# Where x's transposed tiles come from: TensorE transposes of the centred tile, or a DMA that adds a stored transposed layout onto a broadcast of negative means

## The chip, the cores and the metric

The kernel runs on one core of one Trainium2 chip, in one launch. The metric is device time in microseconds, the median of several runs. Beside it there is one profiled execution with its trace. Engines are named as in the profile: PE is TensorE's matmul side and PEld its weight loads, DVE is VectorE, ACT is ScalarE, POOL is GpSimd, SP is the engine that here only issues DMAs. "SPq" or "ACTq" stands for the queue of an engine that issues DMAs and waits.

## What is computed

x has 2048 rows of 512. Its rows are normalised, and two mixers work on the same normalised rows; their results are added to x:

```python
xn = _layernorm(x, axis=-1)                 # (x - m) / sqrt(v + 1e-5), per row
return x + _A_ref(xn, wqkv, w_phi, wo) + _B_ref(xn, w_in, w_sp, b_sp, w_out)
# A: q, k, v = xn @ wqkv, 32 heads of 16; p = q or k @ w_phi per head;
#    phi = [softmax(p), softmax(-p)]; kv = phi_k^T v; z = sum of phi_k;
#    o = (phi_q kv) / (phi_q z + 1e-6); result o @ wo
# B: z = gelu(xn @ w_in), halves z1 and z2; g = w_sp @ layernorm(z2) + b_sp;
#    result (z1 * g) @ w_out
```

Only the way in which xn reaches TensorE is touched. The mean is subtracted from x ahead of the matmuls; the factor 1/sqrt(v + eps), `r_x`, is applied to their results.

## The kernel before

**Precision.** Every matmul is made in three: each operand is split into a rounded part h (`round_h`, line 47, on ACT) and a rest l (`rest_l`, line 51, on DVE), and `mm3` (lines 53 to 57) adds h·h, h·l and l·h in PSUM. These helpers are used all over the kernel, so lines 47, 51, 55, 56 and 57 stand in the profile for many different steps; the tiles' names tell them apart.

**Rows and stages.** The 2048 rows are 16 tiles of 128, counted 0 to 15; "the fifth tile" is tile 4. The first stage, which ends a little after 200 us, makes for each tile the projections to q, k and v (`proj`, 12 matmuls of 512 columns each), the paired softmax of q and of k on DVE and ACT (`softmax_pair`), the sums over k and v (`add_kv`, where matmuls for several tiles are put together after tiles 3, 7, 11, 13 and 15), and the first half of the gated mixer's input (`z1_raw`, 24 matmuls of 344 columns). Later come the other half with its layer norm, the large product with `w_sp` (`products`), and the output projections. All of that follows the first stage and is not edited.

**How x reaches TensorE.** TensorE contracts over the partitions, so it needs x tiles with the 512 features on the partitions, as four blocks of 128×128. For tile s the steps are, in the kernel before:

- `fetch(s)`, `load_x` (line 179): SP loads 128×512 of x (256 KB) into `xt[s]`, one of XB = 5 buffers.
- `stats` (lines 260, 261): DVE takes mean and variance. `neg_mean` (line 265): POOL makes `nm`, minus the mean, one number for each row. `rstd_of` (lines 92, 93): POOL makes `r_x`.
- `center` (line 269): ACT adds `nm` to the tile, in place. Rows are partitions here, so this is a bias for each partition.
- `transposed` (line 275): PE transposes four blocks into the PSUM tile `pt`, one of the four PSUM buffers of the tag "mm" that the projections use too.
- `split_x` (lines 47 and 51): ACT and DVE read `pt` from PSUM and write the h and l halves of `xT[s]`.

Tiles 0 to 3 are made ahead of the loop, in an order written out by hand. From tile 4 on the loop over s does it: iteration s calls `centered(s + 2)`.

**What sets the order.** Each engine works through its own list in order and waits where an operand is not there. The lists are written before the program runs, by a planner that plays the program through with durations of its own: `TileContext(nc, schedule_with_timeline_sim=True)` in the last lines of the kernel. Among the instructions that it thinks ready on an engine it takes the one that stands first in the program. `tc.issue_after(i)` adds a rule that the instructions in its block come after i on i's engine. So an edit in one place can change the lists everywhere, and a wait that the planner thought shorter stops an engine at that place, with all that is queued behind it. The input `x_t` holds x's tiles already transposed, as (tile, feature in block, block, row); the kernel before takes it as an argument and does not use it.

Of the kernel before, what the change touches and what calls it, by code (L numbers as in the profile page):

```python
# [10 lines left out]
F32 = mybir.dt.float32  # L11
F32R = mybir.dt.float32r
AF = mybir.ActivationFunctionType
ALU = mybir.AluOpType
# [4 lines left out]
P = 128  # L19
S, D, H, DH, FH = 2048, 512, 32, 16, 688  # L20
NT = S // P
ND = D // P
# [6 lines left out]
BL = 32  # L29
EPS_LN = 1e-5  # L30
EPS_DEN = 1e-6
XB = 5
NP = NT // 2
HP, QP = P // 2, P // 4
FP = 3 * P
# [4 lines left out]
def mixer(ctx: ExitStack, tc: tile.TileContext, x, x_t, wv, wqkT, phi_bd, wo, w_in, wst, b_r, w_out, out):  # L40
    nc = tc.nc
    pe, act, dve, pool, sp = nc.tensor, nc.scalar, nc.vector, nc.gpsimd, nc.sync


    def round_h(eng, h, src):
        if eng is act:
            return act.activation(h, src, AF.Copy).ins  # L47
        return eng.tensor_copy(h, src).ins

    def rest_l(l, src, h, eng=None):  # L50
        return (eng or dve).tensor_tensor(l, src, h.bitcast(F32), op=ALU.subtract).ins  # L51
# [18 lines left out]
    def xz_tile(n, dt, name):  # L70
        return xz.tile([P, SL], dt, tag="xz", name=name)[:, :n]

    mid = ctx.enter_context(ExitStack())
    dram = ctx.enter_context(tc.tile_pool(name="dram", bufs=1, space=DRAM))
# [2 lines left out]
    u_d = dram.tile([NT, FU, P], F32, name="u_d")  # L77
    kvT_d = dram.tile([P, D], F32, name="kvT_d")
    zb_d = dram.tile([P, NF], F32, name="zb_d")

    ident = cst.tile([P, P], F32, name="ident")
    make_identity(nc, ident)
# [6 lines left out]
    def rstd_of(mv, r, stats=None):  # L89
        if stats is not None:  # L90
            dve.bn_aggr(mv, stats)
        pool.tensor_scalar_add(mv[:, 1:2], mv[:, 1:2], EPS_LN)
        pool.tensor_tensor(r, mv[:, 1:2], mhalf, op=ALU.pow)
# [52 lines left out]
    def z1_raw(pl, ps, s, bufs):  # L146
        z = pl.tile([P, 2, FC], F32, tag="zf", bufs=bufs, name="z1f")
        for k, p in zproj(ps, s, w1):
            act.activation(z[:, k], p, AF.Copy, scale=r_x[:, s:s + 1])
        act.dma_start(z1_d[s], z.rearrange("p a b -> p (a b)"))  # L150
# [21 lines left out]
    with ExitStack() as p0:  # L172
        res = p0.enter_context(left("p0res", 1))
        wk = p0.enter_context(left("p0wk", 2))
        ps = p0.enter_context(psum("p0ps", 4))

        def load_x(s):
            t = wk.tile([P, D], F32, tag="x", bufs=XB, name="xt")
            sp.dma_start(t, x[s * P:(s + 1) * P, :])
            return t  # L180
# [24 lines left out]
        def fold(i, wT, tiles):  # L205


            for g in range(NG):
                for c in range(ND):
                    for m in range(2):  # L210
                        for r in range(2):
                            rows, cols = slice(r * HP, (r + 1) * HP), slice(m * HP, (m + 1) * HP)
                            ins = pe.matmul(tiles[c // 2][r][cols, c % 2, g], wT[g][rows, c * P + m * HP:c * P + (m + 1) * HP],
                                            bd[rows, g * P + r * HP:g * P + (r + 1) * HP], start=True, stop=True,
                                            skip_group_check=True).ins
            return ins

        def folded(i, tiles, keep=lambda **ins: None, between=lambda: None):
            for k in range(2):
                if k:  # L220
                    between()
                for r in range(2):
                    h, l = (w[:, i, 2 * k:2 * k + 2].rearrange("p c (g a b) -> p c g a b", g=NG, a=2)[:, :, :, r] for w in (wqk_h, wqk_l))
                    keep(act=round_h(act, h, tiles[k][r]))
                    keep(dve=rest_l(l, tiles[k][r], h))

        def fold_tiles(pools):
            return [[pl.tile([P, D], F32, tag=tag, name="fold").rearrange("p (c g b) -> p c g b", c=2, g=NG)
                     for _ in range(2)] for pl, tag in pools]
# [15 lines left out]
        xt, v, rounded, ready = {}, {}, [], []  # L245

        def fetch(s):
            if s < NT:
                xt[s] = load_x(s)

        def split_x(src):
            t = xz_tile(2 * D, F32R, "xT").rearrange("p (a b) -> p a b", a=2)
            xT.append(t)
            src = src.rearrange("p a b -> p (a b)")
            rounded.append(round_h(act, t[:, 0], src))
            return rounded[-1], rest_l(t[:, 1], src, t[:, 0])

        def stats(s, keep=lambda **ins: None):
            st6 = wk.tile([P, 6], F32, tag="st6", name="st6")
            dve.bn_stats(st6, xt[s])  # L260
            keep(dve=dve.bn_aggr(mv_x[:, s], st6).ins)

        def neg_mean(s):
            nm = wk.tile([P, 1], F32, tag="nm", name="nm")
            pool.tensor_scalar_mul(nm, mv_x[:, s, 0:1], -1.0)
            return nm

        def center(s, nm):
            return act.activation(xt[s], xt[s], AF.Identity, bias=nm).ins

        def transposed(s):
            xs = xt.pop(s)
            pt = ps.tile([P, ND, P], F32, tag="mm", name="pt")
            for c in range(ND):
                ins = pe.transpose(pt[:, c], xs[:, c * P:(c + 1) * P], ident).ins
            return pt, ins

        def centered(s):
            stats(s)
            nm = neg_mean(s)  # L280
            rstd_of(mv_x[:, s], r_x[:, s:s + 1])
            with tc.issue_after(rounded[s - 2]):
                center(s, nm)
            split_x(transposed(s)[0])

        def keep_v(s, p):
            v[s] = wk.tile([P, D], F32, tag="v", bufs=4, name="v")
# [2 lines left out]
        def proj_v(s):  # L290
            keep_v(s, proj(s, wv_h, wv_l))
# [4 lines left out]
        def proj_k(s):  # L296
            er = spare[s].rearrange("p a b -> p (a b)")[:, :NF + 2 * H] if s in spare else None
            return softmax_pair(wk, proj(s, wqk_h[:, 1], wqk_l[:, 1]), "k", r_x[:, s:s + 1], er=er)

        def proj_q(s):  # L300
            e = softmax_pair(wk, proj(s, wqk_h[:, 0], wqk_l[:, 0]), "q", r_x[:, s:s + 1])
            pool.dma_start(e_d[s], e)

        def add_kv(s, er):

            e = er[:, :NF]
            dve.tensor_tensor(heads(e), heads(e), bc(er[:, NF:], 2 * H), op=ALU.mult)
            pool.dma_start(zacc, e, accum_op=ALU.add)
            ready.append((v.pop(s), e))
            if s not in RUNS:  # L310
                return
            first = s == RUNS[0]
            with ExitStack() as later:
                n = len(ready)
                while ready:
                    vs, e = ready.pop()
                    for m in range(H // 2):
                        k = m % 4 * QP
                        i = pe.matmul(kv_acc[k:k + QP, m // 4], vs[:, m * QP:(m + 1) * QP], e[:, m * HP:(m + 1) * HP],  # L319
                                      start=first and m < 4 and len(ready) == n - 1, stop=s == NT - 1 and not ready,  # L320
                                      skip_group_check=True).ins
                    later.enter_context(tc.issue_after(i))
# [17 lines left out]
        def keep(**ins):  # L340
            for i in ins.values():
                queue.enter_context(tc.issue_after(i))
# [17 lines left out]
        nm = neg_mean(1)  # L360
# [12 lines left out]
        def split_t(pt):  # L373
            i, j = split_x(pt)
            keep(act=i, dve=j)


        t = xz_tile(2 * D, F32R, "xT").rearrange("p (a b) -> p a b", a=2)
# [8 lines left out]
        for cs, pt in zip(halves, pts):  # L387
            src = pt.rearrange("p a b -> p (a b)")
# [23 lines left out]
        def settled(s):  # L412
            stats(s, keep)
            nm = neg_mean(s)
            rstd_of(mv_x[:, s], r_x[:, s:s + 1])
            return nm

        nm = settled(2)
# [4 lines left out]
        nm = settled(3)  # L423
# [24 lines left out]
        keep(pe=zproj.last)  # L448
        spare.update(zip((2, 3, 4, 5, 8, 9), [bd_t] + wkT_t + wqT_t[:1] + w1r))
        n1, nq = 1, 0  # L450
        for s in range(NT):
            fetch(s + 4)
            er = ek[s] if s < len(ek) else proj_k(s)
            if 1 < s < NT - 2:
                centered(s + 2)
            while nq < (s - 2) * NT // (NT - 3):
                proj_q(nq)
                nq += 1
            add_kv(s, er)
            if s == 0:  # L460
                tiles = fold_tiles(((za, "z"), (ps, "mm")))
                keep(pe=fold(0, wqT, tiles))
                folded(0, tiles)
            elif s == 1:
                proj_v(3)
            elif 2 < s < NT - 1:
                proj_v(s + 1)
            while n1 < s * (NT - LAG) // (NT - 1):
                z1_raw(wk, za, n1, 2)
                n1 += 1  # L470
            if s == 3:
                queue.close()
# [330 lines left out]
    for n in range(NC):  # L803
# [27 lines left out]
        if n == NC - 2:  # L831
            es[0], es[1] = first_q(0), first_q(1)
            t = xz_tile((KF + 1) * P, F32R, "u1")
# [10 lines left out]
    wk = ctx.enter_context(left("cwk", 2))  # L844
# [187 lines left out]
```

## Time and profile before

| | us |
|---|---|
| median of 3 runs | 629.55 |
| lowest and highest run | 628.14, 629.68 |
| the profiled execution's own time | 627.78 |
| its span, first to last instruction | 626.1 |
| PE busy | 619.1 (99%) |
| DVE busy | 508.8 (81%) |
| ACT busy | 280.7 (45%) |
| POOL busy | 104.8 (17%) |

The span is what the views of the trace divide up; the profiled execution's own time is 1.7 us more. It lies 1.77 us under the median of the runs. The granted clock of TensorE is 0.999 over the span. Busy shares are averages over stages that have different limits, so a stage is read from its own stretch of the trace.

### The profile page before, as it was taken

The page shows a single profiled execution, that of the slowest core. Times are in us where ns is not written, and L with a number is a line of the kernel's source. Part 1 is how long each engine was busy: PE and PEld are TensorE (multiplying, and loading weights), DVE is VectorE, ACT ScalarE, POOL GpSimd, SP SyncE. Part 2 cuts the span into 40 slices and gives each one's busy share as a digit, 9 for nine tenths or more (in the row PEclk, how much of TensorE's full clock was granted, in tenths as well). Part 3 has the DMA queues.
Part 4 walks back from the last instruction along what each step waited for, and adds up shares of the span by engine and source line. Part 5 has one row for each costly group of instructions (what it writes and reads, how often), then busy time and mean ns, then how long its engine had stood idle before and what let it go on. Part 6 is the DMA issues. An engine that isn't in the chain of part 4 may idle for free.

```text
span 626.1 us, 11429 instructions
## 1 busy us (share of the span) xinstructions
PE 619.1 (99%) x4406; PEld 565.3 (90%) x4406; DVE 508.8 (81%) x893; ACT 280.7 (45%) x446; POOL 104.8 (17%) x187
## 2 busy tenths in 40 slices
PE   8999999999999999999999999999999999999996
PEld 7888888888888999999999999999999877788775
DVE  5999998987988398989898897696978899989211
ACT  5653434443333367877434444243445433334331
POOL 4142122111011015442000000000000212211110
PEclk9999999999999999999999999999999999999999
DMA  9445465354336868001454845637367799984722
GB/s 313 164 109 144 121 156 155 88 143 136 104 93 173 274 234 285 2 2 35 147 115 147 193 96 153 136 119 175 88 174 232 224 297 330 320 249 97 180 34 51
DMA packets 87590, 98.40 MB, mean 157 GB/s; under 512 B 46560, under 2 KB 59616, under 8 KB 87296
## 3 DMA queue, kind: packets, MB, share of 16 engines
q1 hardware_dynamic: 75200, 58.12, 32.4%
q0 software_dynamic: 10032, 33.92, 20.7%
q10 hardware_dynamic: 2304, 5.64, 2.4%
q8 instruction: 34, 0.56, 0.4%
q14 instruction: 20, 0.16, 0.1%
HBM read 56.37 MB, written 30.54 MB: 139 GB/s over the span
## 4 chain that ended last, share of the span: by engine, by line
PE 98%; DVE 0%; ACT 0%; POOL 0%; issue 0%; DVEq 0%; POOLq 0%
PE g L57 11%; PE g L56 11%; PE g L55 11%; PE proj L57 7%; PE proj L55 7%; PE proj L56 7%; PE zps L57 6%; PE zps L55 6%; PE zps L56 6%; PE pout L55 5%; PE pout L57 5%; PE pout L56 5%; PE ptq L890 1%; PE po L905 1%; PE kvps L319 1%; PE pout L919 1%
## 5 line engine op out<-in xcount | busy, mean ns | idle before, releaser
L56 PE MATMUL g<-B,A 128*128 128x344 f32 x448 | 143.3, 320 | 0.0
L55 PE MATMUL g<-B,A 128*128 128x344 f32 x448 | 142.8, 319 | 0.0
L57 PE MATMUL g<-B,A 128*128 128x344 f32 x448 | 140.6, 321 | 0.1
L55 PEld LDWEIGHTS g<-B,A 128*128 128x128 f32 x448 | 84.3, 188 | 0.0
L56 PEld LDWEIGHTS g<-B,A 128*128 128x128 f32 x448 | 84.2, 188 | 0.0
L57 PEld LDWEIGHTS g<-B,A 128*128 128x128 f32 x448 | 83.6, 188 | 0.4 <-DVE A L51 0.4
L47 ACT ACTIVATE A<-S 128x512 fp32r<-128x512 f32 x64 | 39.4, 630 | 71.3 <-DVE S L542 51.3
L55 PE MATMUL proj<-wqk_h,xT 128*128 128x512 f32 x128 | 50.6, 395 | 0.0
L57 PE MATMUL proj<-wqk_h,xT 128*128 128x512 f32 x128 | 50.2, 393 | 0.0
L56 PE MATMUL proj<-wqk_l,xT 128*128 128x512 f32 x128 | 49.9, 390 | 0.0
L47 ACT ACTIVATE A<-wf 128x512 fp32r<-128x512 f32 (+1 forms) x64 | 33.2, 521 | 36.3 <-DMA wf<-in_wst 14.3
L119 ACT ACTIVATE e<-e,r_x 128x1024 f32<-128x1024 f32 x26 | 29.9, 1150 | 40.2 <-DVE e L118 39.6
L51 DVE TENSOR_TENSOR A<-S,A 128x512 fp32r<-128x512 f32 x64 | 43.1, 686 | 4.8 <-ACT A L47 4.3
L55 PE MATMUL zps<-w_0h,xT 128*128 128x344 f32 x128 | 41.4, 323 | 0.0
L57 PE MATMUL zps<-w_0h,xT 128*128 128x344 f32 x128 | 41.0, 320 | 0.0
L55 PE MATMUL zps<-w_1h,xT 128*128 128x344 f32 x128 | 40.9, 320 | 0.0
L57 PE MATMUL zps<-w_1h,xT 128*128 128x344 f32 x128 | 40.7, 319 | 0.0
L56 PE MATMUL zps<-w_0l,xT 128*128 128x344 f32 x128 | 40.6, 317 | 0.0
L56 PE MATMUL zps<-w_1l,xT 128*128 128x344 f32 x128 | 40.6, 317 | 0.0
L51 DVE TENSOR_TENSOR A<-wf,A 128x512 fp32r<-128x512 f32 (+1 forms) x64 | 35.0, 549 | 2.6 <-ACT A L47 2.4
L707 POOL DMA_DIRECT2D z1t<-z_d x16 | 8.7, 547 | 165.5 <-DMA u_d<-z1t 98.7
L122 DVE TENSOR_REDUCE sm<-e 128x64 f32<-128x1024 f32 x26 | 31.4, 1207 | 5.1 <-ACT e L119 5.0
(205 smaller groups left out, 1432.7 us busy)
## 6 DMA issues: line engine op xcount, KB each, us to landing
wf<-in_wst SPq DMA_DIRECT2D x64, 256.0 KB, 3.4
e_d<-e POOLq DMA_DIRECT2D x16, 544.0 KB, 4.6
et<-e_d SPq DMA_DIRECT2D x16, 544.0 KB, 6.4
er<-et POOLq DMA_DIRECT2D x12, 512.0 KB, 6.4
z_d<-z1f ACTq DMA_DIRECT2D x16, 344.0 KB, 2.6
z1t<-z_d POOLq DMA_DIRECT2D x16, 344.0 KB, 5.2
zacc<-e POOLq DMA_DIRECT2D x10, 512.0 KB, 4.7
u<-u_d SPq DMA_DIRECT2D x15, 320.0 KB, 5.6
```

The lines of the kernel that those rows point to most:

```text
L47: return act.activation(h, src, AF.Copy).ins
L51: return (eng or dve).tensor_tensor(l, src, h.bitcast(F32), op=ALU.subtract).ins
L55: pe.matmul(dst, ah, bh, start=start, stop=False)
L56: pe.matmul(dst, ah, bl, start=False, stop=False)
L57: return pe.matmul(dst, al, bh, start=False, stop=stop).ins
L119: act.activation(e, e, AF.Exp, scale=scale)
L122: dve.tensor_reduce(sm, heads(e), axis=AX.X, op=ALU.add)
L319: i = pe.matmul(kv_acc[k:k + QP, m // 4], vs[:, m * QP:(m + 1) * QP], e[:, m * HP:(m + 1) * HP], start=first and m < 4 and len(ready) == n ...
L707: pool.dma_start(t[:, k, :FH], z1_d[2 * i + k])
L890: pe.transpose(pt[:, a, k].bitcast(F32R), src, ident_r)
L905: lasts[3] = pe.matmul(po[r][c * QP:(c + 1) * QP, k], kvT[rows, m // 2, cols], fs[m // 4][rows, m // 2 % 2], start=True, stop=True).ins
L919: lasts[2] = pe.matmul(p, rt, w, start=False, stop=i == NT - 1 and k == 1).ins
```

## The change

For tiles 4 to 15, x is no longer centred and transposed on the engines. DVE takes the statistics as before. SP stores the 128 negative means of a tile in a row of the DRAM tensor `nm_d`. A second SP DMA reads that row back and writes it to all 128 partitions and all four blocks of a new tile `xc[s]`, 128×512. POOL then issues a DMA that adds the stored transposed layout `x_t[s]` onto `xc[s]`. ACT and DVE split `xc[s]` from SBUF. The buffers of `xt` go from 5 to 3, and `xc` has two. `center_t(s + 4)` runs in iteration s, two iterations ahead of its `split_x`, and its statistics are put after the last `rest_l` of `split_x` on DVE. The loads of x are called one iteration earlier. Tiles 0 to 3 are made as before.

```diff
-XB = 5
+XB = 3
...
+    nm_d = dram.tile([NT, P], F32, name="nm_d")
...
             rounded.append(round_h(act, t[:, 0], src))
-            return rounded[-1], rest_l(t[:, 1], src, t[:, 0])
+            split_x.last = rest_l(t[:, 1], src, t[:, 0])
+            return rounded[-1], split_x.last
...
-        def centered(s):
-            stats(s)
+        xc = {}
+
+        def center_t(s):
+
+            with tc.issue_after(split_x.last):
+                stats(s)
+            xt.pop(s)
             nm = neg_mean(s)
             rstd_of(mv_x[:, s], r_x[:, s:s + 1])
-            with tc.issue_after(rounded[s - 2]):
-                center(s, nm)
-            split_x(transposed(s)[0])
+            sp.dma_start(nm_d[s].unsqueeze(1), nm)
+            xc[s] = wk.tile([P, ND, P], F32, tag="xc", name="xc")
+            sp.dma_start(xc[s], nm_d[s].unsqueeze(0).unsqueeze(0).to_broadcast([P, ND, P]))
+            pool.dma_start(xc[s], x_t[s], accum_op=ALU.add)
...
+        fetch(4)
         for s in range(NT):
-            fetch(s + 4)
+            fetch(s + 5)
             er = ek[s] if s < len(ek) else proj_k(s)
             if 1 < s < NT - 2:
-                centered(s + 2)
+                split_x(xc.pop(s + 2))
+            if s < NT - 4:
+                center_t(s + 4)
```

## The prediction

> **What bounds the kernel now.** I read the page's engine totals first, then a table by stretch for the first stage and what follows it, then the chain of work that ended last.
>
> ```profile
> PE 619.1 (99%) x4406; PEld 565.3 (90%) x4406; DVE 508.8 (81%) x893; ACT 280.7 (45%) x446; POOL 104.8 (17%) x187
> ```
>
> ```profile
> 25.00:60.00 35.00, 35.00 (x417) 30.80 (x415) 34.85 (x60) 16.52 (x25) 11.77 (x26) 1.00 0.48 112
> 60.00:100.00 40.00, 40.00 (x201) 34.56 (x200) 37.98 (x59) 15.92 (x21) 8.92 (x18) 1.00 0.47 133
> ...
> 230.00:300.00 70.00, 70.00 (x445) 70.00 (x444) 61.34 (x125) 52.55 (x80) 29.05 (x50) 1.00 0.28 94
> ```
>
> ```profile
> 25.00:205.00 180.00, 180.00 (x1503) 156.66 (x1501) 163.02 (x245) 72.31 (x96) 36.11 (x67) 1.00 0.47 129
> ```
>
> The columns are the stretch, its length, then busy time of PE, PEld, DVE, ACT and POOL with instruction counts, granted clock, DMA share and GB/s. From 25 to 205 us, where the change acts, PE is busy in all of the 180 us: TensorE is the limit, at full clock. DVE has 163.02 of 180, so 17 us to spare, but nearly none early: 34.85 of 35 up to 60 us, and 2.0 of 40 free up to 100. DMA is at half. From 230 to 300 us PE is again busy throughout, and over the whole span it idles for only 626.1 − 619.1 = 7 us. So PE time taken out of the first stage comes off the end, as long as PE stays fed, and little more than that can be won.
>
> **What is removed: 48 transposes.** For twelve tiles four transposes each go. What they cost PE is read from the start times, not from the durations.
>
> ```profile
> 87.85 0.39 PE L56 MATMUL proj<-wqk_l,xT 128*128 128x512 f32 x1
> 88.08 0.40 PE L57 MATMUL proj<-wqk_h,xT 128*128 128x512 f32 x1
> 88.31 0.60 PE L275 MATMUL pt<-ident,xt 128*128 128x128 f32 x4
> 88.67 0.48 PE L55 MATMUL proj<-wqk_h,xT 128*128 128x512 f32 x1
> 88.98 0.39 PE L56 MATMUL proj<-wqk_l,xT 128*128 128x512 f32 x1
> ```
>
> Matmuls of 512 columns start every 0.23 us (87.85, 88.08). From 88.08 to 88.98 two such steps and the four transposes pass: 0.90 − 2×0.225 = 0.45 us, part of it the slower first matmul behind them. The chain that ended last puts 0.44 us on each quartet, first and last of the twelve:
>
> ```profile
> 38.13 0.44 PE pt L275 x4
> ...
> 165.59 0.44 PE pt L275 x4
> ```
>
> So the saving is 12 × 0.45 = 5.4 us of PE time, all of it on the limiting path.
>
> ```profile
> L275 PE MATMUL pt<-ident,xt 128*128 128x128 f32 x60 | 9.0, 272 | 0.0
> L47 ACT ACTIVATE xT<-pt 128x512 fp32r<-128x512 f32 x15 | 8.9, 594 | 19.7 <-PE pt L275 19.7
> L51 DVE TENSOR_TENSOR xT<-pt,xT 128x512 fp32r<-128x512 f32 x15 | 10.1, 672 | 1.9 <-ACT xT L47 1.9
> L269 ACT ACTIVATE xt<-xt,nm 128x512 f32<-128x512 f32 x15 | 10.6, 713 | 0.5 <-POOL mv_x L92 0.5
> L47 ACT ACTIVATE wv_h<-wrow 128x512 fp32r<-128x512 f32 x4 | 2.4, 628 | 0.2 <-DMA wrow<-in_wv 0.2
> L51 DVE TENSOR_TENSOR wv_l<-wrow,wv_h 128x512 fp32r<-128x512 f32 x4 | 2.7, 688 | 0.1
> ```
>
> One transpose lasts 272 ns by its own row, but the next starts well before it ends. The Trainium skill, "TensorE: Matmul & The Clock Gate", Part 4, gives about 275 ns for a 128×128 transpose in one kernel's context; the duration here agrees, and priced by it 48 would be 13.2 us. Here four of them with the weight load behind delay the next start by 0.36 us (88.31 to 88.67), so the pitch decides, not the duration.
>
> Twelve centrings of 0.713 us leave ACT, 8.6 us of an engine that is busy 72 of 180: no gain of its own. The split reads SBUF instead of PSUM; the weight splits from SBUF took 628 and 688 ns against 594 and 672, so 12 × 0.016 = 0.2 us more on DVE, inside its 17 us. DVE does not get less work. A PSUM buffer that was held by each `pt` is free for projections; PE waits for none now, so I count nothing.
>
> **What is added.** Per tile two SP DMAs, one POOL DMA and three transfers, one after the other. Nothing like the 4-byte-per-partition store or the broadcast is in the trace, so I bound them by rows; the columns are the size of one and the median time to landing:
>
> ```profile
> xt<-in_x SPq DMA_DIRECT2D x16, 256.0 KB, 3.9
> wf<-in_wst SPq DMA_DIRECT2D x64, 256.0 KB, 3.4
> zacc<-e POOLq DMA_DIRECT2D x10, 512.0 KB, 4.7
> u<-u_d SPq DMA_DIRECT2D x15, 320.0 KB, 5.6
> out<-xr POOLq DMA_DIRECT2D x15, 256.0 KB, 5.8
> kvT_d<-kvT SPq DMA_DIRECT2D x1, 256.0 KB, 3.3
> wof<-in_wo SPq DMA_DIRECT2D x16, 64.0 KB, 2.8
> bias<-in_b_r SPq DMA_DIRECT2D x1, 8.0 KB, 7.2
> ```
>
> Store of `nm`: between 2.8 (64 KB) and 7.2 us (`bias`, 128 short rows amid the first weights); I take 3.3, the store of `kvT`, also 128 partitions to DRAM. Broadcast: between 3.4 and 5.6 (`u`, whose runs are 512 bytes like these); I take 3.9, the x load of the same size. Adding DMA: between 3.4 (a plain load of the size) and 5.8 (one that adds in DRAM); I take 4.7, `zacc`, which adds in SBUF. Sum 11.9 us, between 9.6 and 18.6. The Trainium skill, "DMA: Bandwidth & Descriptors", "Anatomy of one DMA", gives about 2.0 us plus bytes/436e3 for one DMA; estimated by that, the three would take 2.0 + 2.6 + 2.6 = 7.2 us. That is for GpSimd DMAs by themselves; the 256 KB loads here took 3.4 to 3.9 against its 2.6, so the rows decide.
>
> Does the chain keep PE waiting? The tightest place is the first new tile, because its statistics must now follow the split of tile 3 on DVE.
>
> ```profile
> 28.64 0.68 DVE L51 TENSOR_TENSOR xT<-pt,xT 128x512 fp32r<-128x512 f32 x1
> ```
>
> ```profile
> 45.95 0.39 PE L55 MATMUL proj<-wv_h,xT 128*128 128x512 f32 x1
> ```
>
> ```profile
> 69.76 0.39 PE L55 MATMUL proj<-wv_h,xT 128*128 128x512 f32 x1
> ```
>
> ```profile
> L260 DVE BATCH_NORM_STATS2 st<-xt 128x6 f32<-128x512 f32 x16 | 10.7, 680 | 6.7 <-DMA xt<-in_x 6.7
> L261 DVE BATCH_NORM_AGGREGATE mv_x<-st 128x2 f32<-128x6 f32 x16 | 2.7, 172 | 0.2
> L265 POOL TENSOR_SCALAR nm<-mv_x 128x1 f32<-128x1 f32 x15 | 3.5, 234 | 34.6 <-DVE mv_x L261 24.2 <-ACT xt L269 9.9
> L122 DVE TENSOR_REDUCE sm<-e 128x64 f32<-128x1024 f32 x26 | 31.4, 1207 | 5.1 <-ACT e L119 5.0
> L308 POOL DMA_DIRECT2D zacc<-e x10 | 9.1, 909 | 60.9 <-DVE e L307 30.1 <-DVE e L123 27.4 <-ACT wqk_h L47 2.3
> ```
>
> The first row is the rest of tile 3, which ends at 29.32. From there: statistics 0.68 + 0.17, `nm` 0.23, transfers 11.9, split 0.63 + 0.69 = 14.3, so tile 4 is split at 43.6 us, with the bounds 41.3 and 50.3. PE first uses it in the fifth run of twelve `wv` matmuls, at 45.95, or 45.05 with the two quartets ahead of it gone. So it comes in time by 1.4 us on my values and 5.3 us late at worst, once. I count zero and keep 0 to 5.3 for the range. Afterwards there is room: tile 6 follows tile 4 by the same 14.3 us, at about 58 us, and its `wv` run (the seventh) starts at 69.76. The two buffers of `xc` let odd and even tiles run side by side, so the chain gives a tile every 7 us where PE takes 180/16 = 11.
>
> The queues: SP has nothing in the first stage but the x loads, and each next load is called ahead of the waiting DMAs. With XB = 3 tile 3's load waits for the transposes of tile 0, over at 6.03, and is issued at 10.09 anyway:
>
> ```profile
> 4.97 1.06 PE L384 MATMUL pt<-ident,xt 128*128 128x128 f32 x4
> ```
>
> ```profile
> 10.09 0.33 SPq L179 DMA_DIRECT2D xt<-in_x  x1
> ```
>
> POOL's adding DMA waits for the broadcast, and behind it stand the writes of q's exponentials, the sums into `zacc` and the next tile's `nm` and `r_x`. POOL is busy 36 of 180 us; twelve issues of 0.9 us (as `zacc`'s, the last row above) and twelve waits of at most 3.9 + 3.3 us, if it comes to each straight after `nm`, are 97 us of the 144 free. In its rows it waits for DVE, 30.1 and 27.4 us before the `zacc` sums. Cover: POOL's idle time; without it the k and q buffers would come free late, up to 7 us each. Traffic: 12 × 512 KB in 180 us, 35 GB/s on 129.
>
> **The sum.** 627.78 − 5.4 = 622.4 us for the profiled execution, which stands 1.77 us below the median of its runs; for the median, 629.55 − 5.4 = 624.1 us.
>
> **The rivals.** *ACT stands at the rounding (slower).* The lists are fixed beforehand. If the planner takes the transfers as shorter than they are, ACT stops at `round_h` of `xc` with an exponential queued behind it, and DVE stops at the sum of that exponential. For it: DVE's four waits for an x load in its rows come to 6.7 us, 1.7 us late for each transfer, so some 5 us over three in a row; DVE has no idle time up to 60 us. If DVE bridges 2.4 us of that with another softmax's work, two steps of 1.2 us as the sum `sm` takes, it loses 2.6 us a tile: 163 + 12 × 2.6 = 194 us against 180, +14 us, 644. It cancels the gain from 1.0 us a tile (163 + 12 = 175, PE's new length) and makes it slower from 1.4 on. Against: the steps are called two iterations, 2 × 11 us, ahead of the split, and such waits so far stopped no PE. *The gain is spent on the first tile (no change).* The chain takes its upper bound, PE waits 5.3 us at tile 4 before it can start, 629.4 us; a DVE loss of 1.0 to 1.4 us a tile ends there too. For: only 1.4 us margin, on a store that no row shows. Against: the planner may move other matmuls ahead. *The transposes cost their duration:* 48 × 0.272 = 13.1 us, 616.5. Against: the start times above, and PE has no idle time to hide such a cost.
>
> **How the numbers follow.** About 0.3%, 1.9 us, is what a measurement of this kernel can tell from no change. Forecast 0.62, within 622 to 627. No change or a part of the gain 0.18, of which a quarter is still faster by 1.9 us. ACT's stand 0.18, anywhere from 631 to 645. Full durations 0.02. Faster 0.62 + 0.04 + 0.02 = 0.68, same 0.14, slower 0.18. The range 622 to 634 leaves out the transposes' full price, a little of the forecast's low side, and the upper two thirds of ACT's stand, near 0.16.
>
> **What would show it.** Right: 16 transposes in the rows instead of 64 (four each for tiles 0 to 3), PE still busy throughout from 25 us on, its total down by about 5.4 us, tile 4's `wv` run near 45 us with no idle time ahead, the three transfers near 3.3, 3.9 and 4.7 us, and the stage's last `kvps` matmuls 5 us earlier. Wrong: PE idle before `proj<-wv` waiting for `xT`; ACT waiting for a DMA at line 47 and DVE for ACT in the sums, by more than 1 us a tile; or POOL's wait turning up as DVE's.

## The result and the profile after

The changed kernel takes 753.0 us (median of 5 runs, 750.29 to 753.6) where the kernel before took 628.22 on the same chip: 1.197 times as long, with a 95% interval from 1.195 to 1.199. The forecast was 624.1 us, in a range from 622 to 634. The profiled execution took 751.65 us, its span is 749.9. Three executions further down, one of e7 (741.8 us), one of e9 (1223.4) and the profiled one of e10 (1558.1), were slower than the others of their kernel and are left out of the times, and no landing of e10 is used.

First the engine totals and two rows of the table in 40 slices of the page of the changed kernel. A slice is 18.7 us.

```profile
PE 639.2 (85%) x4358; PEld 576.8 (77%) x4358; DVE 508.1 (68%) x893; ACT 272.2 (36%) x434; POOL 117.0 (16%) x199
...
PE   8936356238249989999999999999999999999997
...
PEclk9978658669758999999999999999999999999999
```

From the third to the twelfth slice, 37 to 225 us, PE is busy for 2 to 8 tenths; from the thirteenth on it runs nearly as before. In the same stretch the granted clock goes down to between 0.5 and 0.9, where before it was full throughout. So PE's total went up by 20 us although 48 matmuls are gone: the same matmuls last longer at a lower clock. That goes with the idling: e4 below, which keeps PE busy in the same stage, has full clock in it. It is taken here as a consequence, because the waits below account for the idling.

The table by stretch, with the columns as before:

```profile
25.00:60.00 35.00, 22.63 (x219) 19.20 (x218) 16.34 (x27) 6.63 (x11) 7.48 (x13) 0.80 0.49 101
60.00:100.00 40.00, 18.74 (x79) 15.97 (x78) 13.76 (x22) 5.35 (x7) 4.85 (x9) 0.75 0.32 58
100.00:200.00 100.00, 52.36 (x315) 42.40 (x313) 38.15 (x62) 14.29 (x19) 15.70 (x26) 0.74 0.54 78
```

From 60 to 100 us PE issues 79 matmuls where it issued 201, and no engine is busy for half of the time: DVE has 13.76 of 40, POOL 4.85. Nothing computes too slowly; everything waits. The groups of instructions and the waits say for what (idle time of the engine ahead of the instruction; in the waits total, times, longest):

```profile
L51 DVE TENSOR_TENSOR xT<-xc,xT 128x512 fp32r<-128x512 f32 x12 | 8.1, 684 | 95.2 <-ACT xT L47 95.2
...
L47 ACT ACTIVATE xT<-xc 128x512 fp32r<-128x512 f32 x12 | 7.3, 626 | 115.6 <-DMA xc<-in_x_t 115.6
```

```profile
POOL xc L292 <- DMA xc<-nm_d: 161.7, 12, 19.4
ACT xT L47 <- DMA xc<-in_x_t: 115.6, 8, 20.6
...
DVE xT L51 <- ACT xT L47: 97.2, 10, 17.5
```

DVE waits for ACT, ACT for the adding DMA, and POOL, which issues that DMA, for the broadcast. The DMA issues (KB each, median us to landing) give the lengths:

```profile
xt<-in_x SPq DMA_DIRECT2D x16, 256.0 KB, 5.3
...
xc<-nm_d SPq DMA_DIRECT2D x12, 256.0 KB, 9.6
xc<-in_x_t POOLq DMA_DIRECT2D x12, 256.0 KB, 4.3
...
nm_d<-nm SPq DMA_DIRECT2D x12, 0.5 KB, 8.2
```

The adding DMA is near its forecast of 4.7, but the store took 8.2 us instead of 3.3 and the broadcast 9.6 instead of 3.9. The chain of work that ended last shows how they stand to one another: first its shares by engine, then two tiles of it in order of time (start, length, what).

```profile
PE 59%; DMA 26%; DVE 8%; issue 4%; POOL 2%; ACT 1%; SPq 0%; POOLq 0%; DVEq 0%; ACTq 0%
```

```profile
74.29 0.24 POOL nm L267
74.53 0.03 issue
74.56 7.70 DMA nm_d<-nm
...
82.34 9.59 DMA xc<-nm_d
91.95 0.04 POOLq L292
...
92.49 0.95 POOL xc L292
93.44 0.08 issue
93.51 0.24 POOL nm L267
...
93.78 9.08 DMA nm_d<-nm
...
102.94 8.75 DMA xc<-nm_d
```

Negative mean, store, broadcast, issue of the adding DMA, and only then the negative mean of the next tile: POOL stands at line 292 until a tile's broadcast has landed, and the next tile's `nm` is behind it in POOL's list. From one `nm` to the next pass 93.51 − 74.29 = 19.2 us, of which store and broadcast are 17.3. The rests of x on DVE follow at that pace: 58.80, 78.24, 97.46, 116.89 and 136.55 us, 19.4 us a tile, where PE needs a tile in 11. The last matmuls of `kvps` end the stage; first the kernel before, then the changed one:

```profile
201.13 1.10 PE L319 MATMUL kvps<-e,v 128*32 128x64 f32 x64
```

```profile
323.91 1.10 PE L327 MATMUL kvps<-e,v 128*32 128x64 f32 x64
```

They start 122.8 us later, so nearly all of the 124 us are lost by then. Behind that point both kernels have the same 2769 matmuls, in 419.9 us of PE's busy time before and 420.6 after.

A closer look at SP's own queue, between two tiles that don't fit that pattern:

```profile
143.64 0.37 SPq L291 DMA_DIRECT2D xc<-nm_d  x1
144.10 0.46 SPq L289 DMA_DIRECT2D nm_d<-nm  x1
158.00 0.37 SPq L291 DMA_DIRECT2D xc<-nm_d  x1
```

Here the next store was ready early and was issued 0.46 us behind a broadcast. It landed after 13.8 us, and SP stood at the next broadcast until then. So the order of transfers on SP is a second suspect beside the loop through POOL.

### The profile page after: what moved, and what is told of

It is laid out like the page before. It is cut to its first block, busy times and chain, and to the rows that moved or that the text cites. A ratio compares the mean times of both kernels' runs of the same rounds, so it can differ in the third digit from the quotient of the medians.

```text
span 749.9 us, 11419 instructions
## 1 busy us (share of the span) xinstructions
PE 639.2 (85%) x4358; PEld 576.8 (77%) x4358; DVE 508.1 (68%) x893; ACT 272.2 (36%) x434; POOL 117.0 (16%) x199
## 3 DMA queue, kind: packets, MB, share of 16 engines
q0 software_dynamic: 11760, 37.07, 21.9%
## 4 chain that ended last, share of the span: by engine, by line
PE 59%; DMA 26%; DVE 8%; issue 4%; POOL 2%; ACT 1%; SPq 0%; POOLq 0%; DVEq 0%; ACTq 0%
DMA xc<-nm_d 11%; DMA nm_d<-nm 10%; PE g L57 9%; PE g L56 9%; PE g L55 9%; PE pout L55 5%; PE pout L57 4%; PE pout L56 4%; PE zps L57 3%; PE zps L55 3%; PE zps L56 3%; DMA e_d<-e 2%; DVE sm L123 2%; DMA zacc<-e 2%; PE ptq L901 1%
## 5 line engine op out<-in xcount | busy, mean ns | idle before, releaser
L55 PE MATMUL proj<-wqk_h,xT 128*128 128x512 f32 x128 | 55.0, 430 | 38.2 <-DVE e L119 15.9
L51 DVE TENSOR_TENSOR xT<-xc,xT 128x512 fp32r<-128x512 f32 x12 | 8.1, 684 | 95.2 <-ACT xT L47 95.2
L55 PE MATMUL proj<-wv_h,xT 128*128 128x512 f32 x64 | 28.8, 450 | 48.5 <-ACT v L296 26.1
L55 PEld LDWEIGHTS proj<-wqk_h,xT 128*128 128x128 f32 x128 | 26.6, 208 | 45.8 <-issue 30.0
L55 PEld LDWEIGHTS proj<-wv_h,xT 128*128 128x128 f32 x64 | 13.7, 214 | 53.5 <-ACT v L296 26.9
L57 PE MATMUL proj<-wqk_h,xT 128*128 128x512 f32 x128 | 53.8, 420 | 0.0
L56 PE MATMUL proj<-wqk_l,xT 128*128 128x512 f32 x128 | 53.6, 419 | 0.0
L55 PE MATMUL zps<-w_1h,xT 128*128 128x344 f32 x128 | 41.7, 326 | 9.3 <-ACT z1f L150 9.3
L47 ACT ACTIVATE xT<-xc 128x512 fp32r<-128x512 f32 x12 | 7.3, 626 | 115.6 <-DMA xc<-in_x_t 115.6
L47 ACT ACTIVATE A<-wf 128x512 fp32r<-128x512 f32 (+1 forms) x64 | 33.3, 521 | 37.8 <-PE g L57 19.4
L118 DVE TENSOR_TENSOR e<-proj,mm 128x512 f32<-128x512 f32 x26 | 17.6, 677 | 43.0 <-DMA e_d<-e 40.6
L55 PE MATMUL zps<-w_0h,xT 128*128 128x344 f32 x128 | 41.2, 322 | 0.8 <-ACT z1f L150 0.8
L57 PE MATMUL zps<-w_1h,xT 128*128 128x344 f32 x128 | 41.4, 325 | 0.0
```

Of the source, the lines that this page charges most:

```text
L55: pe.matmul(dst, ah, bh, start=start, stop=False)
L56: pe.matmul(dst, ah, bl, start=False, stop=False)
L57: return pe.matmul(dst, al, bh, start=False, stop=stop).ins
L118: dve.tensor_tensor(e2[:, :, 0], heads(src), bc(mm[:, 0], H), op=ALU.subtract)
```

## The experiments

Five theories stand in the expectations. In short: (1) POOL's list closes the loop (the next `nm` behind the waiting adding DMA); (2) the split has a bad place in ACT's and DVE's lists; (3) the new traffic by itself slows what else runs; (4) the store and the broadcast are slow and hold one another up on SP's queue; (5) the chain is long and two buffers are too few. In e13 the number 5 stands for another one: the repeated reads hold the DMA engines themselves, whichever queue they came by. Times of the kernel before, on the same chip, were 628.0 to 629.1 us.

**e1: `nm` by DVE, so that POOL's wait no longer holds the next tile.**

```diff
-            pool.tensor_scalar_mul(nm, mv_x[:, s, 0:1], -1.0)
+            (dve if s > 3 else pool).tensor_scalar_mul(nm, mv_x[:, s, 0:1], -1.0)
```

> The changed kernel, with the negative mean of tiles 4 to 15 made by DVE instead of POOL; nothing else is edited. Theory 1 (one chain): in the changed kernel POOL's list holds the next tile's negative mean behind the adding DMA, which waits for the broadcast, so store, broadcast and add of all tiles run one after another, 19.4 us a tile (rests at 78.24, 97.46, 116.89, 136.55). With the mean off POOL two chains of about 25 us run side by side, 12 to 13 us a tile, so 7 us less for each of twelve tiles: about 670 us (650 to 690). Theory 2 (place in the lists): ACT and DVE stand at the split because it is listed too early; that place stays, so 740 to 755 us. Theory 3 (traffic): the added transfers slow all DMA; they stay, so 745 to 755 us.

744.4 us, 1.186 [1.182, 1.189]. The loop through POOL was opened and 9 us came back: by itself it isn't the cause. SP takes its place, as its timeline in this kernel shows:

```profile
183.75 0.37 SPq L291 DMA_DIRECT2D xc<-nm_d  x1
184.22 3.07 SPq L289 DMA_DIRECT2D nm_d<-nm  x1
202.09 0.37 SPq L291 DMA_DIRECT2D xc<-nm_d  x1
```

A store issued 0.47 us behind a broadcast, and the next broadcast 17.9 us later. Tiles now come in pairs, still about 19.5 us for one.

**e2: the split listed later on ACT and DVE.**

```diff
-                split_x(xc.pop(s + 2))
+                with tc.issue_after(softmax_pair.exp), tc.issue_after(softmax_pair.rec):
+                    split_x(xc.pop(s + 2))
```

> The changed kernel, with the split of a tile listed after the exponential of k on ACT and its reciprocal on DVE in the same iteration, so that ACT and DVE have less queued behind the wait for it. The negative mean stays on POOL. Theory 1 (one chain): the tiles come no sooner, 19 us apart, so 740 to 760 us. Theory 2 (place in the lists): the waits of ACT (115.6 us in 8) and DVE (97.2 us in 10) at the split shrink to less than a third and most of the 125 us comes back: under 680 us. Theory 3 (traffic): 745 to 755 us.

746.3 us, 1.188 [1.184, 1.192]. ACT's wait for the adding DMA is still 107.6 us in 11. The place in the lists that was tried gives 7 us back; it isn't the main cause.

**e4: one plain load of `x_t[s]`, no mean.**

```diff
-            nm = neg_mean(s)
-            sp.dma_start(nm_d[s].unsqueeze(1), nm)
-            sp.dma_start(xc[s], nm_d[s].unsqueeze(0).unsqueeze(0).to_broadcast([P, ND, P]))
-            pool.dma_start(xc[s], x_t[s], accum_op=ALU.add)
+            sp.dma_start(xc[s], x_t[s])
```

> The changed kernel with one SP load of the stored transposed tile (256 KB) in place of negative mean, store, broadcast and adding DMA. It leaves out the subtraction of the mean for tiles 4 to 15. All theories: no chain is left, so this is what the removed transposes are worth: 12 x 0.45 = 5.4 us less than the kernel before, about 623 us (620 to 626). If transposes cost PE their duration, 13 us less, about 615 us. If the new lists or the smaller x buffers cost something by themselves, 628 us or more.

623.3 us, 0.9925 [0.990, 0.995]: 4.7 us faster than before. Its row of the table by stretch:

```profile
25.00:205.00 180.00, 180.00 (x1488) 157.16 (x1487) 165.96 (x251) 67.10 (x90) 35.13 (x56) 1.00 0.54 150
```

PE is busy throughout at full clock, and its total is 613.5 us, 5.6 under the 619.1 before. This is the prediction's gain of 5.4 us without its transfers; 13 us, the transposes at their full duration, are refuted.

**e3: no store; the broadcast reads a row of the input, so it waits for nothing. e6: the same, but 512 runs of 512 bytes from addresses of their own.** Both leave `nm` out.

```diff
e3: -            sp.dma_start(xc[s], nm_d[s].unsqueeze(0).unsqueeze(0).to_broadcast([P, ND, P]))
    +            sp.dma_start(xc[s], x_t[s, 0, 0, :].unsqueeze(0).unsqueeze(0).to_broadcast([P, ND, P]))
e6: +            sp.dma_start(xc[s], x_t[s].rearrange("p c t -> (p c) t").rearrange("(c p) t -> p c t", c=ND))
```

> The changed kernel without the negative means and their store; the broadcast reads a row of 128 numbers of the input x_t instead of nm_d, with the same pattern of 512 runs of 512 bytes, and the adding DMA stays. It leaves out the subtraction of the mean for tiles 4 to 15 (they get another row of x added). Theory 1 (one chain): the broadcast waits for no statistics and for no store, broadcast and add of two tiles run side by side, under 11 us a tile, so most of the loss is gone: 620 to 640 us. Theory 2 (place in the lists): ACT still stands for what the planner has too short on two transfers, 650 to 700 us. Theory 3 (traffic): 512 KB a tile still move, so over 700 us. The broadcast's landing, 9.6 us in the changed kernel, says whether the row just stored makes it slow: then under 6 us here; if the pattern does, 8 us or more.

> The kernel without a store (659 us, broadcast 9.6 us to landing), with the same 512 runs of 512 bytes a tile, but each read from an address of its own in x_t instead of all from one row of 512 bytes. It leaves out the subtraction of the mean for tiles 4 to 15 (they get another arrangement of x added). If reading one row 512 times makes the broadcast slow, the landing falls to 4 to 5.6 us (u's load with runs of that size took 5.1 to 5.6) and the kernel takes 622 to 640 us. If the short runs make it slow, 9 us or more and 650 to 665 us.

e3: 659.3 us, 1.049 [1.046, 1.051]: 94 us come back, but the time lies in the range of theory 2 (650 to 700), not of theory 1 (620 to 640). e6: 632.1, 1.005 [1.004, 1.006], as expected; its split has the same place in the program as e3's, so theory 2 doesn't explain e3's rest. The DMA issues, e3 first:

```profile
xt<-in_x SPq DMA_DIRECT2D x16, 256.0 KB, 8.7
...
xc<-in_x_t SPq DMA_DIRECT2D x12, 256.0 KB, 9.6
```

```profile
xt<-in_x SPq DMA_DIRECT2D x16, 256.0 KB, 4.1
...
xc<-in_x_t SPq DMA_DIRECT2D x12, 256.0 KB, 4.2
```

Number and size of the pieces, queue and destination are the same; only in e3 all 512 read one row. That takes 9.6 us instead of 4.2, and the x loads behind it on SP 8.7 instead of 4.1. It is worth 27 us of the kernel. The adding DMA and the short runs are worth the 8.8 us from e4 to e6.

**e5: the store stays, the broadcast reads an input row and doesn't wait for it.** The mean is left out of the result.

```diff
-            sp.dma_start(xc[s], nm_d[s].unsqueeze(0).unsqueeze(0).to_broadcast([P, ND, P]))
+            sp.dma_start(xc[s], x_t[s, 0, 0, :].unsqueeze(0).unsqueeze(0).to_broadcast([P, ND, P]))
```

> The changed kernel with the negative means stored as there, but the broadcast reads a row of the input x_t, so that nothing waits for the store to land; store and broadcast stay on SP's queue. It leaves out the subtraction of the mean for tiles 4 to 15 (another row of x is added). Theory 1 (dependent chain): the 8 us of the store count only because the broadcast waits for it; without the wait the time is that of the kernel without a store, 659 us (650 to 670). Theory 4 (queue): store and broadcast each hold SP's DMA queue, 8 and 9.6 us one behind the other, 17.6 us a tile whatever waits; so 730 to 755 us. Theory 2 (place in the lists): near the kernel without a store, 650 to 680 us.

689.9 us, 1.097 [1.094, 1.099], between theory 1 (650 to 670) and theory 4 (730 to 755). Its landings:

```profile
xt<-in_x SPq DMA_DIRECT2D x16, 256.0 KB, 9.0
...
xc<-in_x_t POOLq DMA_DIRECT2D x12, 256.0 KB, 9.3
...
nm_d<-nm SPq DMA_DIRECT2D x12, 0.5 KB, 11.7
```

A store of 512 bytes for whose landing no broadcast waits costs 31 us over e3; that the broadcast waits for it costs the other 63 us up to 753. The slowing isn't confined to SP's queue: the adding DMA, on POOL's, lands in 9.3 us where e3 has 5.8. SP's order has a part in it too: SP stands at the store until POOL has made `nm`, behind its adding DMA (`nm` at 73.30 us, the store at 73.56), and the next broadcast comes after the store.

**e7: the kernel before, with its transposes, and beside them the store and a broadcast into a tile that nobody reads.** One x buffer makes room for that tile.

```diff
-XB = 5
+XB = 4
+            sp.dma_start(nm_d[s].unsqueeze(1), nm)
+            sc = wk.tile([P, ND, P], F32, tag="sc", bufs=1, name="sc")
+            sp.dma_start(sc, nm_d[s].unsqueeze(0).unsqueeze(0).to_broadcast([P, ND, P]))
```

> The kernel before with PE transposes and ACT centring, with four x buffers instead of five, and with the store of the negative mean and its broadcast into a tile that nobody reads added to SP for tiles 4 to 15. Theories 1, 2 and 4: no engine waits for them, so the time is that of before, 628 us (625 to 632); the landings show what the two cost without a waiting kernel around them: if 8 and 9.6 us again, these durations are their own. Theory 3 (traffic): over 640 us.

734.8 us, 1.166 [1.161, 1.171]. By the expectation this speaks for the slowing of other work, but not as I had meant it: it comes by SP's list and queue. A wait and three rows of the chain of this kernel:

```profile
DVE st L261 <- DMA xt<-in_x: 115.0, 9, 35.9
```

```profile
128.26 10.42 DMA xt<-in_x
...
141.69 7.96 DMA nm_d<-nm
...
150.19 10.76 DMA xt<-in_x
```

The x load is queued on SP behind a broadcast that itself stood there until the store had landed. SP gives a tile every 150.19 − 128.26 = 21.9 us, so the statistics wait for x. This run settles that nothing in the split, in ACT's list or in the depth of `xc` is needed for the loss: the two transfers on SP suffice for +106 us. The one x buffer less isn't tested by itself; e14, which has four too, keeps PE busy for all of the 180 us.

**e9 and e10: e4 with a store that nobody reads, of 128 times 4 bytes (`nm`) or of 128 times 512 bytes.** Like e4 they leave the mean out.

```diff
e9:  +            nm = neg_mean(s)
     +            sp.dma_start(nm_d[s].unsqueeze(1), nm)
e10: +            sp.dma_start(big_d[s], xc[s][:, 0])
```

> The kernel with the plain load of the transposed tile (623.3 us), plus the store of the 128 negative means of each tile as 128 pieces of 4 bytes, which nobody reads and nothing waits for. It leaves out the subtraction of the mean for tiles 4 to 15. Theory 4 (queue): the store lands in about 8 us here too, and loads queued behind it on SP land later; since nothing waits for the store, the kernel takes 623 to 640 us (the unlinked store beside the broadcast cost 31 us). If the store's 8 us were made by the broadcasts around it, it lands in 3 us here and the time is 623 to 625 us.

> The kernel with the plain load of the transposed tile, plus a store of one 128x128 block of each tile (64 KB, 128 pieces of 512 bytes), which nobody reads. It leaves out the subtraction of the mean for tiles 4 to 15. If the 4-byte pieces make the store of the means slow, this one, with 128 times the bytes in as many pieces, lands in about 3 us and the time is 623 to 627 us. If the number of pieces or a store to DRAM as such makes it slow, it lands in 8 us.

e9: 634.4 us, 1.010 [1.008, 1.012], 11.1 us over e4. e10: 626.8, 0.998 [0.996, 1.000], 3.5 us over e4 with 128 times the bytes. In e9:

```profile
xt<-in_x SPq DMA_DIRECT2D x16, 256.0 KB, 5.9
...
nm_d<-nm SPq DMA_DIRECT2D x12, 0.5 KB, 8.6
```

So the store is slow with no broadcast near, and the x loads on the queue go from e4's 3.9 to 5.9 us. The loads into `xc` take up to 10.7 us where e4 has at most 6.3, and ACT waits for them for 19.0 us instead of 6.8. One engine did wait for the store: POOL stood for 10.9 us, in 2 waits, until one had landed, before it wrote the next `nm` into its buffer. So the 11.1 us belong to the late loads and to this wait together.

**e11: 128 reads of the row instead of 512.** The broadcast fills one block of 128×128, `x_t[s]` is loaded plainly, POOL adds the block to it.

```diff
-            sp.dma_start(xc[s], nm_d[s].unsqueeze(0).unsqueeze(0).to_broadcast([P, ND, P]))
-            pool.dma_start(xc[s], x_t[s], accum_op=ALU.add)
+            sp.dma_start(xc[s], x_t[s])
+            nmb = wk.tile([P, P], F32, tag="nmb", bufs=1, name="nmb")
+            sp.dma_start(nmb, nm_d[s].unsqueeze(0).to_broadcast([P, P]))
+            pool.tensor_tensor(xc[s], xc[s], nmb.unsqueeze(1).to_broadcast([P, ND, P]), op=ALU.add)
```

> The changed kernel with the broadcast cut to one block (128 reads of the row of 512 bytes instead of 512), a plain SP load of the transposed tile, and POOL adding the block to the tile's four blocks from SBUF in place of the adding DMA; x buffers two. Nothing is left out of the result. If the time of the broadcast goes with the number of reads of one row, it lands in about 2 us plus a quarter of the rest, 4 us, instead of 9.6, and SP's queue has 8 + 4 us a tile instead of 17.6: 640 to 690 us. If it does not, 730 us or more.

697.6 us, 1.111 [1.108, 1.113], a little above what I expected.

```profile
nmb<-nm_d SPq DMA_DIRECT2D x12, 64.0 KB, 4.5
```

A quarter of the reads takes 4.5 us instead of 9.6, and 55 us come back; as the adding DMA is gone here too, the 55 aren't shown to be the reads' alone. The store and the wait for it remain.

**e13: e1 with the broadcast on POOL's queue** (`pool.dma_start` in place of `sp.dma_start` in that line). **e15: the changed kernel with a third buffer of `xc`, two of x and each chain begun an iteration earlier. e16: e13 with the same.**

```diff
-            xc[s] = wk.tile([P, ND, P], F32, tag="xc", name="xc")
+            xc[s] = wk.tile([P, ND, P], F32, tag="xc", bufs=3, name="xc")
...
+        center_t(4)
+        fetch(5)
...
-            if s < NT - 4:
-                center_t(s + 4)
+            if s < NT - 5:
+                center_t(s + 5)
```

> The version with the negative mean on DVE (744.4 us), with the broadcast issued from POOL's DMA queue instead of SP's. Nothing is left out of the result. Theory 4 (SP's queue): a store or an x load issued behind a broadcast waits in the same queue for it (stores of 13.3 and 17.8 us to landing in that version); on another queue it does not, so stores land in about 8 us throughout, two chains of 25 us run side by side, and the time is 670 to 710 us. Theory 5 (the DMA engines): reading one row 512 times holds the engines themselves, whichever queue it came by; stores still land in 13 us or more behind a broadcast and the time stays at 730 to 755 us.

> The changed kernel with a third buffer of xc, and each tile's chain begun one iteration earlier (the x buffers go to two, to make room). All transfers stay on the queues that the change gave them. Theory 4 (SP's queue takes the store and the broadcast of a tile one after the other, and each waits for the one before, so about 19 us a tile pass whatever the number of buffers): no gain, 735 to 765 us, and tiles' rests on DVE still 18 to 20 us apart. Theory 5 (the chain is long and there are only two buffers for it): three tiles in the time of two, 13 us a tile instead of 19.4, which over twelve tiles takes 75 us or so off, 660 to 700 us.

> The kernel of e13 (negative means by DVE, broadcast issued on POOL's queue, only the store and the x loads on SP's) with a third buffer of xc and each chain begun one iteration earlier. Theory 5 (after the queues are parted, what is left is that a pair of tiles goes through its transfers and its waits in the lists in 33 us, and two buffers hold no more than a pair): three tiles in 33 us are 11 us a tile, as PE takes, so the loss falls to the shorter part, 640 to 670 us. Theory 4 (the transfers themselves take the time, one broadcast of 9.4 us behind the other's store): 700 to 730 us, no more than 20 us off e13's 722.

e13: 722.4 us, 1.148 [1.145, 1.150], between the theories: 22 us better than e1. Its stores land in 6.9 to 9.4 us, as theory 4 has it, except one of 14.7 us that had a broadcast on POOL's queue under way for most of its time. So parting the queues helps, and whether the DMA engines hold the rest is open. e15: 760.8, 1.213 [1.209, 1.218]. e16: 714.2, 1.137 [1.134, 1.140]. More depth gains nothing on SP's queue and 8 us on two queues: too few buffers isn't the main cause. In e15 the store still goes out only after the broadcast of the tile before, and the rests still follow at 77.09, 96.74 and 116.44 us. In e16 the wait stands on POOL's queue instead:

```profile
91.59 0.83 POOL L291 DMA_DIRECT2D xc<-nm_d  x1 [6.12 <-DMA nm_d<-nm]
92.41 0.92 POOL L316 DMA_DIRECT2D zacc<-bd  x1
93.22 0.90 POOL L291 DMA_DIRECT2D xc<-nm_d  x1
100.33 0.85 POOL L292 DMA_DIRECT2D xc<-in_x_t  x1 [6.22 <-DMA xc<-nm_d]
105.45 0.85 POOL L292 DMA_DIRECT2D xc<-in_x_t  x1 [4.26 <-DMA xc<-nm_d]
```

POOL stands for the store, then for one broadcast, then for the other. Eight rests from 61.35 to 152.23 us are 13.0 us apart: better than 19.4, still over PE's 11.

**e8: the means without a trip through DRAM.** SP loads `x_t[s]` plainly. One PE transpose of `nm`, read with step 0 along 128 columns, puts the row of negative means on all partitions of a PSUM tile, and DVE adds it.

```diff
-            sp.dma_start(nm_d[s].unsqueeze(1), nm)
-            sp.dma_start(xc[s], nm_d[s].unsqueeze(0).unsqueeze(0).to_broadcast([P, ND, P]))
-            pool.dma_start(xc[s], x_t[s], accum_op=ALU.add)
+            sp.dma_start(xc[s], x_t[s])
+            pb = ps.tile([P, P], F32, tag="mm", name="pb")
+            pe.transpose(pb, nm.to_broadcast([P, P]), ident)
+            dve.tensor_tensor(xc[s], xc[s], pb.unsqueeze(1).to_broadcast([P, ND, P]), op=ALU.add)
```

> A version without the DRAM round trip: SP loads the stored transposed tile, one PE transpose of the negative mean (one column read 128 times) makes its broadcast in PSUM, and DVE adds it to the tile; nothing is left out of the result. PE saves three transposes of four and pays one, 12 x 0.34 = 4 us less; DVE gets 12 adds of 0.69 us, 8.3 us of its 17 us of idle time. If DVE's idle time covers them: 624 us (623 to 626). If not, early on where DVE has none: 627 to 633 us.

626.9 us (12 runs), 0.9972 [0.9956, 0.9989]: the only complete version that beats the kernel before, by 0.3%, which is about the least that can be told from no change here. It lies between its two expectations. The table by stretch:

```profile
25.00:60.00 35.00, 34.55 (x297) 30.72 (x296) 34.97 (x59) 14.31 (x23) 11.62 (x21) 1.00 0.59 156
25.00:205.00 180.00, 179.55 (x1481) 156.22 (x1480) 168.87 (x257) 65.83 (x87) 38.72 (x67) 1.00 0.53 148
```

Three of four transposes are saved, and PE loses 0.45 us where DVE is full, 34.97 of 35 up to 60 us. That is less than the 2.5 us that are missing from the expected 4; the rest is open.

**e12: the same with a copy by ACT and the add by POOL. e14: the same for tiles 8 to 15 only,** tiles 4 to 7 as before.

> The version with the broadcast of the negative mean by one PE transpose (626.9 us), with ACT copying it to SBUF and POOL adding it to the tile instead of DVE; x buffers two. Nothing is left out of the result. DVE loses 12 adds of 0.68 us that it has no idle time for in its first 35 us: 623 to 626 us. If POOL's adds, which share time with its DMA issues, or the smaller x buffers delay the split: 627 to 632 us.

> A version in which tiles 4 to 7 are centred by ACT and transposed by PE as before the change, and tiles 8 to 15 take the stored transposed tile with the negative mean broadcast by one PE transpose and added by DVE (as in the 626.9 us version for all twelve). Four x buffers, one of xc; nothing is left out of the result. PE saves 8 x 0.34 = 2.7 us, and DVE's eight adds fall after 60 us, where it has idle time: 625 to 626 us. If the place where DVE lacks time is not what cost the other version its gain: 627 us or more.

Both were meant to spare DVE early, and both lost: 633.6 us, 1.008 [1.007, 1.010], and 633.0, 1.007 [1.005, 1.009]. In e12 PE is busy for 177.17 of the 180 us from 25 on. In e14 it is busy for all of them and misses 2.35 us from 205 to 300, behind the edit. The lists there were planned anew; why they are worse is open.

## Why the prediction was wrong

**Right.** TensorE bounded the kernel before, and 48 transposes are worth about 0.11 us each by the forecast, 5.4 us, and 0.10 by e4, 4.7 us. The split from SBUF fits in DVE's spare time (165.96 of 180 in e4, PE unharmed). The adding DMA takes 4.3 us where 4.7 were forecast.

**The step that failed** is "The two buffers of `xc` let odd and even tiles run side by side, so the chain gives a tile every 7 us where PE takes 180/16 = 11." Nothing let them: each tile's `nm` stood on POOL behind the wait for the broadcast of the tile before, and once that was mended (e1), store and broadcast stood in line on SP. Nearly all of a tile's steps before its split run one tile after the other, and the length of that loop is the pace: measured 19.2 us against the 7 that were forecast. The prediction named both facts in its next paragraph (POOL's adding DMA "waits for the broadcast, and behind it stand … the next tile's `nm`", and both transfers on SP) and priced them as idle time of POOL. With its own values the loop is nm 0.23, store 3.3, broadcast 3.9 and issue 0.9, together 8.3 us, still under 11; with its own upper bounds, 0.23 + 7.2 + 5.6 + 0.9 = 13.9, over PE's 11.25 by 2.7 us a tile, some 32 us slower. The bounds were carried to the first tile only, as 5.3 us "once". That tile itself was forecast at 43.6 us, with 50.3 as the bound; its rest ended at 55.66 (54.97 + 0.69).

**Two terms were mis-sized, beyond their bounds.** The store: 2.8 to 7.2 us, measured 8.2, and 13 to 18 behind a broadcast. Its likeliest value came from `kvT`, which has as many partitions but whole rows in them; the one row of short pieces, `bias` with 7.2, was put down to its surroundings. The broadcast: 3.4 to 5.6, measured 9.6. All its rows read each byte once; none read one row 512 times, and e6 shows that this is the difference.

**The queues.** "SP has nothing in the first stage but the x loads, and each next load is called ahead of the waiting DMAs": in e7 and in the changed kernel the load after that one is issued behind a broadcast, and lands late. Being called ahead of one wait does not help against a queue that needs 19 to 22 us a tile.

**The rivals.** "ACT stands at the rounding" has its signature in the profile, 115.6 us in 8 waits, but as a consequence: it was priced at 14 us as a matter of lists and steps, and the later place that e2 tries gives 7 us back. (Of its span, 631 to 645 us, the part above 634 is 11/14, not the two thirds of the prediction's reckoning.) "The transposes cost their duration" is refuted by e4.

**The account,** by leaving out one thing after another: 753.0 to e3's 659.3 for the store and the wait for it, 93.7 us (31 of them with no broadcast waiting for it, by e5); to e6's 632.1 for 512 reads of one row, 27.2; to e4's 623.3 for the adding DMA and short runs, 8.8; and e4 is 4.7 under the kernel before. The parts depend on this order: in the linked chain a shorter broadcast, together with a plain load for the adding DMA, gave 55 us (e11). What of the store's part is SP's list, its queue and the DMA engines is not separated: e13 shows only that another queue for the broadcast gives 22 us back.

## What to carry to other kernels

Before a chain of transfers is called hidden, draw its loop: what of the next tile stands behind a wait of this one, on each issuing engine and each DMA queue; the sum around that loop, at the upper bounds, against the bound engine's time for a tile decides, not the latency of one chain divided by the buffers. A transfer that the trace has no equal of, in the length of its pieces and in how often it reads an address, should be given a wider bound than the rows of its size, or measured by itself first. One number per partition that is wanted along the free axis on all partitions is better turned on TensorE (0.27 us in e8) than sent through DRAM (17.3 us).

## What the runs showed of the hardware that I had not expected

- 512 pieces of 512 bytes that all read one row of DRAM land in 9.6 us, 128 such reads in 4.5, and 512 pieces from addresses of their own in 4.2. The Trainium skill, "DMA: Bandwidth & Descriptors", "Anatomy of one DMA", gives 2.0 us plus bytes/436e3 for GpSimd's DMAs, by estimate 2.6 us for 256 KB. On SP's queue here distinct reads come to 4.2 and repeated ones to 9.6. Why the repetition costs is open.
- A store of 128 pieces of 4 bytes takes 8.2 us (after) to 8.6 (e9, e11) and costs a kernel in which no transfer waits for it 11.1 us, against 3.5 for 128 pieces of 512 bytes. The Trainium skill, "DMA: Bandwidth & Descriptors", "Specifications", says that transfers under 512 bytes are done by reading, changing and writing back. That agrees in direction; no run here shows the mechanism.
- A transfer issued within half a microsecond behind a broadcast on SP's queue lands late: an x load in 9.0 to 9.8 us (after) and 10.1 to 10.8 (e7) against 3.9 before, a store of 512 bytes in 13.8 (after) and 13.3 to 17.8 (e1) against 8.2. With the broadcast on POOL's queue the stores landed in 6.9 to 14.7 us, with a median of 7.9 (e13), and in 6.9 to 12.4 with a median of 9.0 (e16).
- POOL's add of 128×512 with an operand repeated over the blocks took 1.26 us in e11 and 1.33 in e12, about twice DVE's 0.68 in e8, where that operand lay in PSUM.
